# One core, retention feeding a hypermixer: another order of loads, steps, engines and banks, pair 4 loaded in 256-byte rows, and the last half pair projected in two column halves

## The chip, the core and the metric

The kernel runs on one core of one Trainium2 chip. The core has five engines that run side by side, each with a queue of its own: TensorE (PE, with its weight loads shown apart as PEld), VectorE (DVE), ScalarE (ACT), GpSimd (POOL) and SyncE (SP, which here only issues transfers). The metric is the time of one execution on the device, in microseconds. The kernel before took 95.64 us, the median of three runs (94.63 to 96.15).

## The reference

Two parts follow each other. With B = 4 batches, H = 8 heads, S = 768 steps and D = 64, the first is a linear attention with a decaying state, the second a token mixer on its result, which has 512 columns (8 heads of 64):

```python
gamma = 1.0 - 2.0 ** (-5.0 - np.arange(H))
for t in range(S):
    state = gamma * state + einsum('bhd,bhe->bhde', k[:, :, t], v[:, :, t])
    y[:, :, t] = scale * einsum('bhd,bhde->bhe', q[:, :, t], state)
x = y.transpose(0, 2, 1, 3).reshape(B, S, H * D)
wq, wk = x @ w_q, x @ w_k                       # 512 -> 64
W_tok = scale * einsum('bsd,btd->bst', wq, wk)
mixed = einsum('bst,btd->bsd', W_tok, x)
out = np.maximum(mixed, 0.0) @ w_out            # 512 x 512
```

Inputs and output are float32; the engines compute in bfloat16 with float32 sums.

## The kernel before, in words

The 4 x 768 tokens are cut into 12 **pairs** of two chunks of 128 tokens, three pairs to a batch. Each pair goes through the same steps, and every step is a small function (L450 to L981) named by two or three letters:

- **Loads** (`load`, L157): q, k and v of a pair, 512 KB each, into a pool of 16 staging buffers. A pair of type "1" has k and v loaded by one transfer each, two tokens in a row of 512 bytes; a pair of type "n" by two transfers each, one for each chunk, a token of a head in a row of 256 bytes. q comes in rows of 2 KB. `TYPES` (L63) gives each pair's type. SP issues the loads in the order of `LOADS` (L58); a load waits until the cast that reads its buffer's last content, 16 loads back, is done (`more_loads`, L227). `w` holds w_q and w_k, `o0` and `o1` the halves of w_out. `s3` stores pair 3's output, `s9/1` chunk 1 of pair 9; the stores all stand behind the loads.
- **Casts to bfloat16**: `ck`, `cv` (with the decay factors), `cq`. For type "1" each half of a chunk is an instruction on 64 partitions, two for a chunk; for type "n" one instruction on 128. [...]
- **Transposes** on PE, `trk`, `trq`, `xt`, and their evictions `ek`, `eq`, `exT`. Where `HALVED` (L64) has a 1, a transpose is made as two halves of 64 rows into two banks of PSUM in place of one.
- **Attention**: `sc` (q times k, two halves of the heads), `eat` (evict under the causal mask, on DVE), `ia` (masked scores times v), `in` (q times the state of before), `st` and `es` (state update and its eviction), `ex` (evict x).
- **Mixer**: `wk`, `wq`, `ew` (x times w_k and w_q, evicted), `zm`, `ez` (sum of wk times x over a batch, evicted: so the rest of a batch waits for its last pair), `mx`, `r` (wq times that sum, and the relu), `pj`, `eo` (times w_out, evicted to the output buffer). The last pair, 11, is in `SPLIT`: most of its steps run for each chunk apart.

`ORDER` (L16) writes the whole program out by hand: 430 tokens such as `sc.3.1@5` (pair 3, half 1, into bank 5 of the 8 PSUM banks) or `ek.5:V` (on DVE; A is ACT, P is POOL). Each engine runs its own tokens in that order; between engines only data and buffers make one wait. `fill.8@6` are 8 matmuls of 512 columns on zeros, which keep PE busy where it would wait. `W` and `WO.0`, `WO.1` cast the weights; `pj` needs both `WO`.

The diff touches the tables at the top, `pj` (L963), `eo` (L975), `stored` (L985) and the first loads (L220).

Of the kernel before, what the change touches and what calls it, by code (L numbers as in the profile page):

```python
# [64 lines left out]
TWO_WQ = "0000"  # L65
DECAYED_Q = "000000111001"
# [993 lines left out]
```

## Time and profile before

| | us |
|---|---|
| median of three runs | 95.64 |
| profiled execution, its own time | 95.0 |
| its span in the profile | 93.3 |
| PE busy | 85.2 |
| DVE busy | 72.7 |
| ACT busy | 67.4 |
| POOL busy | 65.1 |

A profile's line "L966 PE MATMUL banks<-wout_sb,relu" is a group: line 966 of the kernel, on PE, reading tiles wout_sb and relu and writing PSUM (the tile `banks`). A row of a timeline has the start, the duration, the engine, the line, the operation, and in brackets how long the engine sat idle ahead of it and for what. "SPq" is SP's queue: the issue of a transfer, waits of the queue included. Releasers are inferred, and a wait for several things is put down to the one that came last. A matmul's end is modelled, so the time between the starts of two groups on PE says more than a group's own duration; the chain of work (start, duration, engine, line, number of matmuls) cuts PE's time up without overlap.

### The profile page before, as it was taken

What the parts mean: (1) busy time and instruction counts of PE and PEld (TensorE: products, weight loads), DVE (VectorE), ACT (ScalarE), POOL (GpSimd) and SP (SyncE); (2) the same over time, 40 slices, a digit from 0 to 9 for tenths busy, and PEclk for the clock granted to TensorE, in tenths of its full rate; (3) what the DMA queues carried; (4) which work ended last, traced back from release to release, by engine and by line L of the source; (5) the groups of instructions that cost most, each with busy time, mean ns of one, the idle gap of its engine ahead of it and who ended that gap; (6) DMA issues with size and microseconds to landing.
All of it is one profiled execution on the core that took longest, in us unless ns stands there. A gap on an engine that the chain in (4) does not pass through costs nothing.

```text
span 93.3 us, 3399 instructions
## 1 busy us (share of the span) xinstructions
PE 85.2 (91%) x1406; PEld 55.4 (59%) x1420; DVE 72.7 (78%) x116; ACT 67.4 (72%) x107; POOL 65.1 (70%) x84
## 2 busy tenths in 40 slices
PE   4997999898999999999999999999999999999940
PEld 1353566656887764578777557768774586744410
DVE  4869679979899999798798978988898894433730
ACT  4284479995969989877949889888678598367220
POOL 7879699999999999999998699978559500000000
PEclk9999999999999999999999999999999999999999
DMA  1999999999999999897998996998999999935683
GB/s 22 264 376 379 358 369 332 274 311 359 370 372 348 339 262 314 228 258 176 303 207 241 359 291 134 317 241 234 274 209 296 403 404 400 399 120 202 263 313 122
DMA packets 43567, 26.69 MB, mean 286 GB/s; under 512 B 22560, under 2 KB 36896, under 8 KB 43552
## 3 DMA queue, kind: packets, MB, share of 16 engines
q1 hardware_dynamic: 43024, 26.22, 92.8%
q10 hardware_dynamic: 528, 0.26, 0.9%
q8 instruction: 11, 0.18, 0.7%
q14 instruction: 4, 0.03, 0.1%
HBM read 20.19 MB, written 6.29 MB: 284 GB/s over the span
## 4 chain that ended last, share of the span: by engine, by line
PE 66%; SPq 15%; DMA 7%; DVE 4%; issue 2%; ACT 2%; DVEq 0%
PE banks L966 23%; DMA q_st<-in_q_dram 7%; SPq L186 6%; PE banks L594 6%; PE banks L826 5%; SPq L164 5%; PE banks L697 5%; PE banks L665 4%; PE banks L802 4%; SPq L202 4%; PE banks L878 3%; PE banks L514 3%; PE banks L651 3%; DVE x_nat L740 3%; PE banks L770 2%; PE banks L569 2%
## 5 line engine op out<-in xcount | busy, mean ns | idle before, releaser
L467 POOL TENSOR_TENSOR vs<-v_st,fv 64x512 bf16<-64x512 f32 x26 | 28.1, 1082 | 2.5 <-DMA v_st<-in_v_dram 1.0
L966 PE MATMUL banks<-wout_sb,relu 128*128 128x512 bf16 x85 | 22.5, 380 | 0.8 <-issue 0.3
L608 DVE TENSOR_TENSOR at_sb<-banks,cmask 128x1024 bf16<-128x1024 f32 x14 | 16.6, 1220 | 1.5 <-PE banks L594 0.9
L148 ACT COPY o_st<-banks 128x512 f32<-128x512 f32 x21 | 12.3, 589 | 7.3 <-PE banks L966 7.1
L608 DVE TENSOR_TENSOR at_sb<-banks,cmask_n 128x1024 bf16<-128x1024 f32 x10 | 12.0, 1221 | 1.9 <-PE banks L594 1.1
L149 POOL CAST ks<-k_st 64x512 bf16<-64x512 f32 (+1 forms) x20 | 12.1, 609 | 1.6 <-DMA k_st<-in_k_dram 1.0
L966 PEld LDWEIGHTS <-relu 128*128 128x128 bf16 x96 | 8.1, 98 | 8.5 <-DVE relu L961 0.5
L148 ACT CAST s_sb<-banks 128x512 bf16<-128x512 f32 x17 | 10.0, 586 | 3.2 <-PE banks L665 3.0
L444 PE MATMUL banks<-warm 128*128 128x512 bf16 x33 | 10.6, 453 | 1.6 <-DVE warm L253 1.3
L148 ACT CAST ks<-k_st 64x512 bf16<-64x512 f32 (+1 forms) x16 | 9.9, 620 | 2.4 <-DMA k_st<-in_k_dram 2.3
L740 DVE TENSOR_TENSOR x_nat<-banks,fy 128x1024 bf16<-128x1024 f32 x8 | 9.8, 1222 | 2.1 <-PE banks L697 1.2
L959 ACT ACTIVATE relu<-banks 128x1024 bf16<-128x1024 f32 (+1 forms) x11 | 10.2, 946 | 0.9 <-PE banks L938 0.9
L488 POOL TENSOR_TENSOR vs<-v_st,fn_n 128x512 bf16<-128x512 f32 x8 | 8.2, 1042 | 1.9 <-DMA v_st<-in_v_dram 1.9
L594 PE MATMUL banks<-qT,kT 64*128 64x128 bf16 x192 | 9.2, 218 | 0.2 <-DVE x_nat L740 0.2
L534 POOL TENSOR_TENSOR qs<-q_st,fq 128x1024 bf16<-128x1024 f32 x4 | 7.6, 1911 | 1.0 <-DMA q_st<-in_q_dram 1.0
L149 DVE COPY kT<-banks 128x1024 bf16<-128x1024 bf16 x11 | 7.6, 688 | 0.9 <-PE banks L514 0.7
L594 PEld LDWEIGHTS <-kT 64*128 64x128 bf16 x192 | 5.6, 94 | 4.3 <-issue 2.2
L697 PE MATMUL banks<-vs,at_sb 128*128 128x64 bf16 x176 | 7.8, 194 | 0.1
L665 PE MATMUL banks<-vs,ks 128*128 128x128 bf16 x80 | 7.8, 220 | 0.0
L149 DVE COPY xT<-banks 128x1024 bf16<-128x1024 bf16 (+1 forms) x10 | 6.3, 634 | 1.8 <-PE banks L768 1.3
L697 PEld LDWEIGHTS <-at_sb 128*128 128x128 bf16 x176 | 6.3, 98 | 2.1 <-issue 0.6
L148 ACT CAST wqk_n<-banks 128x384 bf16<-128x384 f32 (+1 forms) x12 | 5.5, 470 | 2.3 <-PE banks L826 2.0
(88 smaller groups left out, 140.9 us busy)
## 6 DMA issues: line engine op xcount, KB each, us to landing
q_st<-in_q_dram SPq DMA_DIRECT2D x12, 512.0 KB, 6.8
out_dram<-o_st SPq DMA_DIRECT2D x9, 512.0 KB, 5.2
v_st<-in_v_dram SPq DMA_DIRECT2D x7, 512.0 KB, 6.7
k_st<-in_k_dram SPq DMA_DIRECT2D x6, 512.0 KB, 6.1
k_st<-in_k_dram SPq DMA_DIRECT2D x11, 256.0 KB, 5.1
v_st<-in_v_dram SPq DMA_DIRECT2D x10, 256.0 KB, 5.4
out_dram<-o_st SPq DMA_DIRECT2D x6, 256.0 KB, 2.0
o_st<-in_moe_w_out_dram SPq DMA_DIRECT2D x2, 512.0 KB, 9.4
```

Of the source, the lines that this page charges most:

```text
L148: return nc.scalar.copy(out=out, in_=in_)
L149: return ENGINES[e].tensor_copy(out=out, in_=in_)
L444: nc.tensor.matmul(out=bank32(b), lhsT=warm[:, 0:128], rhs=warm, start=True, stop=True)
L467: ENGINES[e].tensor_tensor(out=st["vs"][rows(j), c].rearrange("p hp x d -> p (hp x) d"), in0=st["v_st"][rows(c), :, :, j].rearrange("p hp ...
L488: ENGINES[e].tensor_tensor(out=st["vs"][:, c].rearrange("p hp x d -> p (hp x) d"), in0=st["v_st"][:, c].rearrange("p hp x d -> p (hp x) d" ...
L594: nc.tensor.matmul(out=ps[:, x, hi, c, :], lhsT=st["kT"][rows(x), hp, c, :], rhs=qT(p, x, hp, c), start=(hi == 0 and c == 0), stop=(hi == ...
L608: ENGINES[e].tensor_tensor(out=st["at", half].rearrange("p x hi i t -> p (x hi i t)").rearrange("p (m n) -> p m n", n=n), in0=st["at_ps", ...
L665: nc.tensor.matmul(out=state_ps(p)[:, hp].rearrange("p x d -> p (x d)"), lhsT=st["ks"][:, c, hp].rearrange("p x d -> p (x d)"), rhs=st["vs ...
L697: nc.tensor.matmul(out=y_of(p, b, c)[:, x, hp, :], lhsT=st["at", half][:, x, hi, c, :], rhs=st["vs"][:, c, hp, x, :], start=first(p, x), s ...
L740: nc.vector.tensor_tensor(out=st["x"].rearrange("p c hp x d -> p x (c hp) d"), in0=st["y_ps", 0].rearrange("p x c hp d -> p x (c hp) d"), ...
L959: nc.scalar.activation(out=dst, in_=src, func=ACT.Relu)
L966: nc.tensor.matmul(out=bank32(b), lhsT=st["relu"][:, c, a, :], rhs=wout_sb[:, a, :], start=(a == 0), stop=(a == NDM - 1),)
```

## The change

It keeps every function's arithmetic. These things differ:

- **ORDER** is another one, of 436 tokens. All steps of before are in it, in other places, many with another bank or engine. `fill` has 34 matmuls for 36. `cq.2`, `cq.7` and `cq.8` are split in halves, and of the two halves of pairs 4 and 8 one runs on DVE. `WO.1` moves from POOL to ACT.
- **LOADS** is another order: k1 ahead of v1, q3 and k3 ahead of w, k5 ahead of q4 and k4, o1 next behind k4; q5 and v4 behind o1.
- **TYPES**: pair 4 is "n" now, so its k and v come in 256-byte rows by four transfers, and its casts are one instruction for each chunk.
- **HALVED**: k for pairs 0, 8, 9, 10, 11 (before 5, 10); q for 0, 5, 8, 10, 11 (before 0, 5, 7 to 11); x for 4, 5, 7 to 10 (before 4, 6, 7, 9 to 11).
- **DECAYED_Q**: pairs 4, 5, 8, 10, 11 (before 6, 7, 8, 11).
- **The last half pair**: `pj.11.0`, `eo.11.0` and the store of pair 11's first chunk are cut into two halves of 256 columns and come last; the second half's store is issued from ACT's queue.
- `FIRST` is a new switch for the first loads, and it is empty, so the first loads stay.

```diff
-mask.0:P mask.2:P fill.13@6 cv.0.1:V ck.0.1:P ck.0.0:A fx:A trk.0@0 ek.0:V cq.0:A fill.8@6 trq.0@1
-eq.0:V fill.4@6 sc.0.1@0 cq.1.0:A cv.0.0:P st.0.0 es.0.0:A sc.0.0@2 fill.2@6 st.0.1 eat.0.1:V
-in.0.1@0 ia.0.1@0 eat.0.0:V cq.1.1:P fill.2@6 ia.0.0@0 ex.0:V trq.1@2 cv.1.1:P ck.1.0:A ck.1.1:P
-trk.1@3 ek.1:V cq.2:A trq.2@6 eq.2:V eq.1:A fill.2@5 sc.1.0@2 eat.1.0:V xt.0@0 sc.1.1@5 es.0.1:A
-cv.1.0:P st.1.0 ck.2.1:A eat.1.1:V ck.2.0:P fill.1@4 trk.2@1 es.1.0:A st.1.1 in.1.0@2 ia.1.0@2
-ek.2:V cv.2.0:P ia.1.1@2 W:A in.1.1@2 es.1.1:A ck.3.0:A ex.1:V sc.2.1@4 eat.2.1:V fill.3@6 sc.2.0@1
-eat.2.0:V cv.2.1:P xt.1@3 ck.3.1:P cq.3:A fill.1@6 st.2.0 es.2.0:A ia.2.1@4 exT.0:A trq.3@6 in.2.1@4
...
-ez.0.0:V mx.0@2 r.0:A mx.2@4 r.2:A ck.4.0:P trq.4@6 ex.3:V xt.3@0 WO.0:P eq.4:V trq.5@1 cv.4.1:P
-exT.3:V eq.5:A trk.4@6 ek.4:V wk.3@0 st.3.1 es.3.1:V mx.1@3 r.1:A sc.4.0@5 eat.4.0:V sc.4.1@1 wq.3
-ew.3:A WO.1:P pj.2.1@3 pj.1.1@0 ck.5.0:A eo.2.1:A eo.1.1:A pj.0.1@6 cv.4.0:P st.4.0 es.4.0:A
...
-pj.10.0@0 mx.10.1@3 r.10.1:V mx.11.1@1 r.11.1:V eo.10.0:A pj.9.0@6 eo.9.0:A pj.10.1@3 eo.10.1:V
-pj.11.1@6 pj.9.1@1 eo.9.1:A eo.11.1:V
+mask.0:P mask.2:P fill.13@6 cv.0.0:V ck.0.0:A ck.0.1:P fx:A trk.0@0 ek.0:V cq.0:A fill.8@6 trq.0@2
+cq.1.1:A cv.0.1:P fill.1@6 st.0.0 es.0.0:A eq.0:V fill.1@6 sc.0.0@1 eat.0.0:V sc.0.1@3 in.0.1@5
+eat.0.1:V cq.1.0:P st.0.1 trq.1@0 ia.0.0@5 ck.1.1:A ck.1.0:P trk.1@1 ek.1:V fill.1@2 ia.0.1@5 ex.0:V
+eq.1:A fill.1@4 sc.1.1@0 eat.1.1:V fill.4@4 xt.0@6 sc.1.0@4 eat.1.0:V cv.1.1:P es.0.1:A ck.2.1:A
+ck.2.0:A trk.2@3 ek.2:V cv.1.0:P cq.2.1:P st.1.0 cq.2.0:A trq.2@0 eq.2:V cv.2.0:P ia.1.0@4 es.1.0:A
+exT.0:A ia.1.1@4 st.1.1 es.1.1:A in.1.1@4 in.1.0@4 fill.1@3 sc.2.0@0 sc.2.1@2 ex.1:V fill.2@6 xt.1@4
+cq.3:A cv.2.1:P fill.2@6 st.2.0 trq.3@5 ck.3.1:A es.2.0:A eat.2.1:V ia.2.1@2 W:A in.2.1@2 in.2.0@2
...
+st.3.0 es.3.0:A zm.2@2 zm.1@2 ez.0.0:A eat.3.1:V cq.4.0:V ia.3.0@3 in.3.1@3 mx.2@1 r.2:A ia.3.1@3
+st.3.1 WO.1:A mx.1@5 ex.3:V r.1:A cq.4.1:P trq.4@0 eq.4:V WO.0:P ck.4.0:P ck.4.1:P trk.4@1 ek.4:V
+xt.3@3 pj.2.1@4 eo.2.1:A exT.3:V sc.4.0@0 ck.5.1:P es.3.1:V mx.0@5 r.0:A eat.4.0:V pj.1.1@2 eo.1.1:A
...
+r.9.1:V pj.9.1@6 eo.9.1:V mx.11.0@1 r.11.0:V mx.11.1@3 pj.10.1@0 eo.10.1:V r.11.1:A pj.11.1@6
+pj.11.0.0@5 eo.11.1:V eo.11.0.0:A pj.11.0.1@1 eo.11.0.1:A
...
-v0 q0 q1 v1 k1 q2 k2 v2 w k3 q3 v3 q4 q5 k4 o0 v4 o1 k5 v5 q6 k6 q7 v6 k7 k8 v7 q8 v8 q9 k9 q11 k11
-v9 q10 k10 v10 v11a v11b s0 s2 s1 s4 s3 s5 s6 s8 s7 s11/0 s10/0 s9/0 s10/1 s11/1 s9/1
+v0 q0 q1 k1 v1 k2 q2 v2 q3 k3 w v3 k5 q4 o0 k4 o1 q5 v4 q6 v5 k6 k8 v6 q7 q8 k7 v7 v8 k9 q9 v9 q10
+k10 q11 k11 v10 v11a v11b s1 s2 s0 s3 s4 s5 s8 s7 s6 s10/0 s9/0 s9/1 s10/1 s11/1 s11/0/0 s11/0/1
...
-TYPES = "111111nn1nnn"
-HALVED = dict(k="000001000010", q="100001011111", x="000010110111")
+TYPES = "1111n1nn1nnn"
+HALVED = dict(k="100000001111", q="100001001011", x="000011011110")
...
-DECAYED_Q = "000000111001"
+DECAYED_Q = "000011001011"
...
-    def pj(e, b, p, c):
+    def columns(half):
+        return slice(0, DM) if half is None else slice(half * DM // 2, (half + 1) * DM // 2)
+
+    def pj(e, b, p, c, half=None):
         st = pairs[p]
+        cols = columns(half)
+        ps = bank32(b)[:, 0 : cols.stop - cols.start]
         for a in range(NDM):
             nc.tensor.matmul(
-                out=bank32(b),
+                out=ps,
                 lhsT=st["relu"][:, c, a, :],
-                rhs=wout_sb[:, a, :],
+                rhs=wout_sb[:, a, cols],
...
-        copy(e, st["o"][:, c], st["o_ps", c])
-        evicted.add((p, c))
+        copy(e, st["o"][:, c, columns(half)], st["o_ps", c, half])
+        evicted.add((p, c, half))
...
-            nc.sync.dma_start(out=out[b, t0 : t0 + C, :], in_=pairs[p]["o"][:, cs[0]])
+            (nc.scalar if half else nc.sync).dma_start(
+                out=out[b, t0 : t0 + C, columns(half)],
+                in_=pairs[p]["o"][:, c, columns(half)],
+            )
```

More of the change, by code (lines that the diff above doesn't have):

```diff
@@ L218, in load_token, with load_chunk @@
             load(token[0], int(token[1:]))
-    load("k", 0, 0, nc.scalar)
-    load("k", 0, 1, nc.sync)
-    queue = list(LOADS)
-    staged = ["k0"]
+    def load_chunk(name, c, eng):
+        st = pairs[0]
+        if name + "_st" not in st:
+            st[name + "_st"] = stage_pool.tile([128, HP, 2, 2, D], FP32, name=name + "_st", tag="st")
+        eng.dma_start(
+            out=st[name + "_st"][rows(c)].rearrange("g hp x j d -> g (hp x) (j d)"),
+            in_={"k": k, "v": v}[name][0, :, c * C : (c + 1) * C, :].rearrange(
+                "h (g j) d -> g h (j d)", j=2
+            ),
+        )
+    if FIRST:
+        for i, piece in enumerate(FIRST.split()):
+            load_chunk(piece[0], int(piece[1]), nc.sync if i else nc.scalar)
+        staged = ["k0", "v0"]
+    else:
+        load("k", 0, 0, nc.scalar)
+        load("k", 0, 1, nc.sync)
+        staged = ["k0"]
+    queue = list(LOADS)[len(staged) - 1 :]
     cast = set()
@@ L972, in pj, with eo @@
             )
-        st["o_ps", c] = bank32(b)
-    def eo(e, b, p, c):
+        st["o_ps", c, half] = ps
+    def eo(e, b, p, c, half=None):
         st = pairs[p]
@@ L985, in stored @@
     def stored(name):
[L986 to L988 removed]
+        p, c, half = ([int(i) for i in name.split("/")] + [None, None])[:3]
+        if not all((p, i, half) in evicted for i in ([0, 1] if c is None else [c])):
             return False
         b, cp = divmod(p, NP)
[L991 to L993 removed]
+        if c is not None:
+            t0 = (2 * cp + c) * C
+            (nc.scalar if half else nc.sync).dma_start(
+                out=out[b, t0 : t0 + C, columns(half)],
+                in_=pairs[p]["o"][:, c, columns(half)],
+            )
         else:
```

58 lines of the change are left out of this document (27 added, 31 removed).

## The prediction

> **What bounds the kernel now.** I read the page first: the span, the busy shares, the slices.
>
> ```profile
> span 93.3 us, 3399 instructions
> PE 85.2 (91%) x1406; PEld 55.4 (59%) x1420; DVE 72.7 (78%) x116; ACT 67.4 (72%) x107; POOL 65.1 (70%) x84
> PE   4997999898999999999999999999999999999940
> DMA  1999999999999999897998996998999999935683
> ```
>
> PE and the DMA queues look full together, DVE comes next. Second, the table of stretches (us, then busy time and count of PE, PEld, DVE, ACT, POOL, clock, DMA share, GB/s), to see how much PE idles once the first loads are in.
>
> ```profile
> 20.00:30.00 10.00, 9.34 (x175) 7.29 (x176) 9.14 (x10) 8.09 (x14) 9.37 (x12) 1.00 1.07 360
> 30.00:40.00 10.00, 9.70 (x154) 6.00 (x154) 9.01 (x11) 9.07 (x14) 9.45 (x10) 1.00 1.01 291
> 40.00:50.00 10.00, 9.86 (x193) 7.46 (x195) 8.81 (x9) 7.39 (x13) 9.74 (x11) 1.00 0.94 218
> 50.00:60.00 10.00, 9.84 (x180) 6.39 (x181) 8.99 (x11) 8.88 (x14) 8.72 (x10) 1.00 1.01 286
> 60.00:70.00 10.00, 9.88 (x233) 7.48 (x231) 8.43 (x10) 7.99 (x14) 7.10 (x8) 1.00 1.02 243
> 70.00:80.00 10.00, 9.74 (x209) 6.68 (x209) 8.01 (x11) 7.41 (x13) 3.63 (x4) 1.00 1.07 377
> ```
>
> From 30 to 80 us PE idles 0.30 + 0.14 + 0.16 + 0.12 + 0.26 = 1.0 us of 50, at full granted clock. So no order can win more than about 1 us there, and any new wait is paid in full. What is left to win is ahead of 22 us, where PE runs filler matmuls, and behind the last matmul.
>
> Third, the loads: SP's queue, the transfer rates in two stretches of one microsecond (10 to 11, rows of 512 bytes; 59 to 60, rows of 256 bytes), and the last load's reader.
>
> ```profile
> DMA packets 681, 0.35 MB, mean 347 GB/s; under 512 B 4, under 2 KB 681, under 8 KB 681
> DMA packets 1095, 0.29 MB, mean 290 GB/s; under 512 B 1087, under 2 KB 1087, under 8 KB 1095
> 23.76 3.90 SPq L206 DMA_DIRECT2D o_st<-in_moe_w_out_dram  x1
> o_st<-in_moe_w_out_dram SPq DMA_DIRECT2D x1, 512.0 KB, 8.9
> 30.41 2.29 SPq L164 DMA_DIRECT2D q_st<-in_q_dram  x1
> 63.58 5.83 SPq L176 DMA_DIRECT2D v_st<-in_v_dram  x4
> 73.30 1.04 POOL L488 TENSOR_TENSOR vs<-v_st,fn_n 128x512 bf16<-128x512 f32 x1 [0.71 <-DMA v_st<-in_v_dram]
> ```
>
> A tensor of one pair (0.524 MB) takes 0.524/0.347 = 1.51 us in rows of 512 bytes and 0.524/0.290 = 1.81 us in rows of 256. From 30.41 to 69.41 SP issues 28 load transfers, one per 1.39 us, whether of 256 or 512 KB. The last one is used as it lands (0.71 us idle ahead of it): the loads are a second bound with almost no slack.
>
> **The change, part by part.** Nearly every step of the order is the same step in another place. I take the places that move the end.
>
> *The front.* DVE leads here; the first four rows are its own, the others PE's.
>
> ```profile
> 10.94 2.36 DVE L608 TENSOR_TENSOR at_sb<-banks,cmask 128x1024 bf16<-128x1024 f32 x2 [0.68 <-PE banks L594]
> 13.87 1.23 DVE L740 TENSOR_TENSOR x_nat<-banks,fy 128x1024 bf16<-128x1024 f32 x1 [0.57 <-PE banks L697]
> 18.61 0.69 DVE L149 COPY kT<-banks 128x1024 bf16<-128x1024 bf16 x1
> 19.86 1.23 DVE L740 TENSOR_TENSOR x_nat<-banks,fy 128x1024 bf16<-128x1024 f32 x1 [0.56 <-PE banks L651]
> 21.13 0.38 PE L594 MATMUL banks<-qT,kT 64*128 64x128 bf16 x7 [0.18 <-DVE x_nat L740]
> 21.45 0.62 PE L770 MATMUL banks<-identity,x_nat 128*128 128x128 bf16 x8
> 21.90 0.38 PE L444 MATMUL banks<-warm 128*128 128x512 bf16 x1
> 22.12 0.39 PE L665 MATMUL banks<-vs,ks 128*128 128x128 bf16 x4
> ```
>
> DVE twice waits for PE, 0.57 and 0.56 us, because PE came late to ia and in behind fills. In the new order k1 is loaded ahead of v1, trq.1 and trk.1 follow sc.0.1 at once, and ek.1 stands ahead of ex.0 on DVE, so it fills the first wait; ek.2 and eq.2 stand together ahead of ex.1 and fill the second. From the end of pair 0's masks (10.94 + 2.36 = 13.30) the new DVE chain is ek.1 0.69, ex.0 1.23, two masks 2.36, ek.2 and eq.2 1.38, ex.1 1.23: 6.89, so ex.1 ends at 20.2. Now it ends at 19.86 + 1.23 = 21.1. Both orders then run xt.1, fills and st.2.0, which is PE's row at 22.12. Now sc.2.0 also waits for ex.1 (0.18 idle, then 0.32 until 21.45); in the new order it has other banks and runs earlier. New: 20.2, xt.1 0.45 (21.45 to 21.90), two fills of 0.22 (21.90 to 22.12): st.2.0 at 21.1, 1.0 us earlier. I take -0.85, leaving 0.15 for handovers. Ends: -1.13 (both waits gone) and -0.44 (only the two fills gone by which the whole order is shorter, 34 for 36).
>
> *Pair 4 and the output weights.* Pair 4's k and v now come as four transfers of 256 KB in 256-byte rows in place of two of 512 KB; o1, the second half of w_out, is asked for after k4. WO.1, its cast, goes from POOL to ACT and stands ahead of r.1 there; trk.4, xt.3 and pj.2.1 stand earlier on PE. Rows of now: the cast, the first projection, an ACT cast of that size, and the steps that pj.2.1 is moved past, from the chain of work.
>
> ```profile
> 33.82 1.04 POOL L149 CAST wout_sb<-o_st 128x1024 bf16<-128x1024 f32 x1
> 34.77 2.76 PE L966 MATMUL banks<-wout_sb,relu 128*128 128x512 bf16 x11
> L148 ACT CAST qs<-q_st 128x1024 bf16<-128x1024 f32 x3 | 3.1, 1046 | 2.1 <-DMA q_st<-in_q_dram 2.0
> 31.91 0.34 PE banks L569 x16
> 32.25 0.55 PE banks L514 x8
> 32.80 0.30 PE banks L802 x8
> 33.32 0.33 PE banks L938 x4
> 33.65 0.56 PE banks L594 x16
> 34.21 0.54 PE banks L826 x4
> ```
>
> pj.2.1 now starts as WO.1 ends, with no wait. The new order takes from ahead of it trq.5 (0.34), wk.3 (0.30), wq.3 (0.54), both sc.4 (0.56) and one mx (4 + 4 matmuls, about 0.45): 2.2 us. PE would be there at 34.77 - 0.85 - 2.2 = 31.7. o1 lands now at 23.76 + 8.9 = 32.66. In the new list q5 and v4 no longer stand ahead of it and k5 does: one tensor less (-1.51), k4 in smaller rows (+0.30), so 31.45; ACT's cast takes 1.05, so wout is there at 32.5. PE waits 0.8 us. Behind WO.1 on ACT stand r.1 and with it mx.0's bank and pj.1.1; sc.4.0 and mx.0 cover r.1's microsecond. I take +0.8; ends 0 (o1 0.8 earlier) and +2.0 (o1 no earlier than now, since it is the 21st transfer in both lists). Of v4: 0.30 more, its reader is later, nothing. The rest of pair 4 saves POOL and ACT instructions, with PE as cover: nothing.
>
> What 256-byte rows cost is 290 against 347 GB/s in the rows above, a sixth. [...]
>
> *PE's own work.* k is transposed in halves for five pairs in place of two, q for five in place of seven, x for six in both. Full and halved k are above and below here (0.55; 0.34), full and halved q likewise (0.62; 0.34).
>
> ```profile
> 23.06 0.62 PE banks L571 x8
> 37.76 0.34 PE banks L510 x16
> ```
>
> 2 x 0.28 - 3 x 0.21 = -0.07: nothing. A halved transpose fills two banks; where the other is still being read it waits, which is in the open term below.
>
> *Engines changed elsewhere.* ACT, POOL and DVE steps are traded (three eq more and two ek fewer on DVE, decayed q halves there, ez all on ACT). Summed by their rows DVE loses about 0.4 us, ACT 1, POOL 2.5. None sets the end as long as PE is fed: nothing, with PE's 1.0 us of idle (30 to 80 us) as the most that could be won, and the loss open.
>
> *The last half pair.* Rows of now: eviction, store, and an ACT eviction of 256 columns.
>
> ```profile
> 89.68 0.59 ACT o_st L148
> 90.30 0.33 SPq L993 DMA_DIRECT2D out_dram<-o_st  x1
> out_dram<-o_st SPq DMA_DIRECT2D x1, 256.0 KB, 2.0
> L148 ACT CAST z_sb<-banks 128x256 bf16<-128x256 f32 x2 | 0.7, 372 | 1.3 <-PE banks L878 1.3
> ```
>
> The two half projections stream the same columns through PE: nothing. The last eviction shrinks from 0.59 to 0.37 (-0.22). The last store has 128 KB for 256; I take 0.13 off its 2.0 us (ends 0 and 0.45), since most of that is not bytes. It is issued from ACT, behind nothing. Chunk 11.1 is evicted on DVE while PE runs the two halves, so its store is not the last. Sum -0.35, ends -0.67 and 0.
>
> **Sum**: -0.85 + 0.8 + 0 - 0.35 = -0.4 us. The profiled execution took 95.0 us (1.7 beyond its span), so 94.6; the median of the runs is 95.64, 1% above that.
>
> **Rivals.**
>
> *B, the loads set the pace (slower).* If a transfer costs its turn of 1.39 us and not its bytes, o1, 21st in both lists, still lands at 32.66, WO.1 ends at 33.7, and PE waits 2.0 us ahead of pj.2.1: 95.0 - 0.85 + 2.0 - 0.35 = 95.8, and later loads come 2 x 1.39 = 2.8 us later, v6 being wanted earlier than now; 1 us lost there gives 96.8. For it: the 1.39 us over 28 transfers, the DMA share near 1. Against: rows of 512 bytes fill the queue at 347 GB/s in the front, where bytes count. It decides from a wait of 1.2 us on there; below that the change is not slower.
>
> *C, the front's gain stays (faster).* o1 lands by 30.7, there is no new wait, and the middle gives back 0.4 of its 1.0 us: 95.0 - 0.85 - 0.35 - 0.4 = 93.4. For it: DVE and POOL have less to do. Against: the loads have no slack, as the 0.71 us at 73.30 shows.
>
> *D, nothing happens.* PE's work is the same within 0.1 us, and gains and waits cancel: 95.0 to 95.6. It lies inside my range and is not told apart from the forecast.
>
> **How the numbers follow.** Forecast with D 0.45, B 0.30, C 0.25. The forecast is 94.6, its own range 93.8 to 95.6. About 2% is what a measurement of this kernel can tell: below 93.7 and above 97.6. Of C four fifths and a little of the forecast are faster: 0.23. Of B about two fifths, and some other lost wait, are slower: 0.15. The rest, 0.62, is the same. The range to hold 8 in 10 goes from C (93.4, with the tail's far end 93.0) to B with a second wait, 96.8.
>
> **What would show it.** DVE's ex.1 (L740) should end near 20.2 and st.2.0 (L665) start near 21.3. A wait of near 0.8 us ahead of the first L966 group, behind ACT's cast of wout_sb, which waits for the DMA of o_st, shows the second step; none there speaks for C, 2 us for B. The last ACT o_st should take 0.37 us with some 3.3 us from PE's end to the span's. PE idle of over 2 us between 35 and 80 us in the table of stretches, or POOL waiting for v_st ahead of pair 6, would make the prediction wrong towards slow.

## The result and the profile after

The changed kernel is slower: 97.12 us median of 20 runs against 95.65 us of 20 runs of the kernel before, a ratio of 1.0127 with the 95% interval 1.0091 to 1.0163. The medians are over all executions, while the ratios, here and below, leave out those that ran slow, so the two need not agree. The difference is under the 2% that the prediction took as what a measurement of this kernel can tell, but its interval lies clear of 1. The forecast was 0.4 us less (94.6 us against the profiled 95.0); 1.0127 x 95.0 = 96.2 us is what came, 1.2 us more. The profiled execution of the changed kernel took 96.14 us with a span of 94.4 us (before: 95.0 and 93.3).

In the line numbers of the changed kernel, the matmuls of `pj` are L990, those of `st` L684, of `sc` L613, of `trk` L533 (L529 in halves); POOL's casts of v are L486 (type "1") and L507 (type "n"); copies are L149 on ACT and L150 on DVE and POOL; `ex` is L759.

First the page of the changed kernel: the span, the busy sums, and from the 40 slices PE, the granted clock and the DMA queues.

```profile
span 94.4 us, 3420 instructions
PE 84.5 (90%) x1415; PEld 56.8 (60%) x1430; DVE 71.8 (76%) x116; ACT 67.2 (71%) x107; POOL 63.4 (67%) x84
PE   4999978999957999999999999999979999999940
PEclk9999999999999589999999999999999999999999
DMA  0999999999998999999999989999989999965863
```

PE's work is the same (84.5 for 85.2 us), the DMA queues are as full as before, and there are two new things in the middle: a 5 and a 7 in PE's slices behind 26 us, and a stretch of lower granted clock behind it. The table of stretches (us, then busy time and count of PE, PEld, DVE, ACT, POOL, clock, DMA share, GB/s), with its sum from 10 to 80 us, shows the size:

```profile
20.00:30.00 10.00, 7.87 (x145) 6.33 (x145) 8.94 (x10) 7.26 (x14) 8.08 (x9) 1.00 0.97 283
30.00:40.00 10.00, 9.89 (x123) 6.40 (x122) 6.92 (x9) 7.09 (x11) 8.68 (x11) 0.83 1.09 297
40.00:50.00 10.00, 9.95 (x229) 7.82 (x230) 9.12 (x12) 8.00 (x14) 8.08 (x10) 1.00 1.06 281
...
60.00:70.00 10.00, 9.31 (x220) 6.92 (x221) 8.40 (x10) 8.40 (x14) 7.13 (x8) 1.00 1.06 259
...
sum 70.00, PE 65.54 PEld 47.53 DVE 58.86 ACT 56.06 POOL 55.20; mean PE 9.36 PEld 6.79 DVE 8.41 ACT 8.01 POOL 7.89
```

The same sum for the kernel before:

```profile
sum 70.00, PE 67.59 PEld 47.58 DVE 60.59 ACT 56.83 POOL 56.74; mean PE 9.66 PEld 6.80 DVE 8.66 ACT 8.12 POOL 8.11
```

PE idles 70 - 65.54 = 4.46 us between 10 and 80 us, where it idled 2.41. (Three of the profiles below that differ little from this order, and that kept the full clock, have 4.2 to 4.7.) The front itself did what was forecast; these are DVE's `ex.1` and PE's `st.2.0`, the rows to hold against 19.86 and 22.12 of before:

```profile
18.85 1.22 DVE L759 TENSOR_TENSOR x_nat<-banks,fy 128x1024 bf16<-128x1024 f32 x1 [0.34 <-PE banks L670]
...
21.02 0.39 PE L684 MATMUL banks<-vs,ks 128*128 128x128 bf16 x4
```

`ex.1` ends at 20.07 and `st.2.0` starts 1.10 us earlier. The gain lasts until 27 us. Rows of SP's queue, POOL and PE in the changed kernel show where it ends:

```profile
16.31 0.67 SPq L203 DMA_DIRECT2D w_st<-in_moe_w_k_dram  x1
17.02 1.55 SPq L187 DMA_DIRECT2D v_st<-in_v_dram  x1
...
24.55 4.35 POOL L486 TENSOR_TENSOR vs<-v_st,fv 64x512 bf16<-64x512 f32 x4 [1.50 <-DMA v_st<-in_v_dram]
...
28.95 0.38 PE L684 MATMUL banks<-vs,ks 128*128 128x128 bf16 x4 [1.77 <-POOL vs L486]
```

And the rows of the kernel before for the same load, casts and `st.3.0`:

```profile
17.28 0.60 SPq L186 DMA_DIRECT2D v_st<-in_v_dram  x1
...
23.74 4.37 POOL L467 TENSOR_TENSOR vs<-v_st,fv 64x512 bf16<-64x512 f32 x4
...
27.90 0.39 PE L665 MATMUL banks<-vs,ks 128*128 128x128 bf16 x4
```

v3 is asked for at the same moment in both (17.02 and 17.28), since the same transfers stand ahead of it. In the kernel before, POOL takes it at 23.74 without a wait. In the changed one POOL is ready at 23.04 and sits 1.50 us until 24.55, and PE waits 1.77 us for POOL. PE ran ahead by 1.1 us; the load did not. Of POOL's 1.50 us, though, only 0.6 are POOL's being ready earlier (23.04 for 23.66). The rest is this load: it landed 7.5 us behind its issue, in the kernel before 6.2. In five other profiles below with the same loads ahead of v3 it landed after 5.5 to 6.7 us, and PE waited 0.35 to 1.04 us at `st.3.0`, so the 1.77 us of this one execution are more than the usual price. The rest of the way the changed kernel shows the same pattern in smaller pieces, at the casts of v6, v9 and q11, and on PE behind q11's:

```profile
44.33 2.04 POOL L507 TENSOR_TENSOR vs<-v_st,fn_n 128x512 bf16<-128x512 f32 x2 [1.10 <-DMA v_st<-in_v_dram]
...
61.43 2.04 POOL L507 TENSOR_TENSOR vs<-v_st,fn_n 128x512 bf16<-128x512 f32 x2 [1.23 <-DMA v_st<-in_v_dram]
...
68.13 1.90 POOL L553 TENSOR_TENSOR qs<-q_st,fq 128x1024 bf16<-128x1024 f32 x1 [1.35 <-DMA q_st<-in_q_dram]
...
70.08 0.41 PE L588 MATMUL banks<-identity_q,qs 64*128 64x64 bf16 x16 [0.51 <-POOL qs L553]
...
66.23 4.99 SPq L177 DMA_DIRECT2D v_st<-in_v_dram  x4
```

The last row is SP's queue: the last loads are issued by 71.22 us, 1.8 us later than before.

### The profile page after: what moved, and what is told of

Same layout as the page of the kernel before. It is cut to its first block, busy times and chain, and to the rows that moved or that the text cites. A ratio compares the mean times of both kernels' runs of the same rounds, so it can differ in the third digit from the quotient of the medians.

```text
span 94.4 us, 3420 instructions
## 1 busy us (share of the span) xinstructions
PE 84.5 (90%) x1415; PEld 56.8 (60%) x1430; DVE 71.8 (76%) x116; ACT 67.2 (71%) x107; POOL 63.4 (67%) x84
## 4 chain that ended last, share of the span: by engine, by line
PE 55%; DMA 16%; POOL 16%; issue 5%; SPq 3%; ACT 0%; POOLq 0%
PE banks L990 21%; POOL vs L486 12%; DMA v_st<-in_v_dram 9%; DMA q_st<-in_q_dram 8%; PE banks L613 4%; PE banks L684 4%; PE banks L716 4%; PE banks L845 3%; PE banks L957 3%; PE banks L897 2%; PE banks L533 2%; PE banks L590 2%; POOL qs L553 2%; PE banks L670 2%; PE banks L821 2%
## 5 line engine op out<-in xcount | busy, mean ns | idle before, releaser
L486 POOL TENSOR_TENSOR vs<-v_st,fv 64x512 bf16<-64x512 f32 x22 | 23.8, 1083 | 3.3 <-DMA v_st<-in_v_dram 2.2
L990 PE MATMUL banks<-wout_sb,relu 128*128 128x512 bf16 (+1 forms) x88 | 22.5, 371 | 0.8 <-issue 0.3
L149 ACT COPY o_st<-banks 128x512 f32<-128x512 f32 (+1 forms) x20 | 11.3, 565 | 6.5 <-PE banks L990 6.2
L627 DVE TENSOR_TENSOR at_sb<-banks,cmask_n 128x1024 bf16<-128x1024 f32 x12 | 14.3, 1214 | 0.8 <-PE banks L613 0.8
L627 DVE TENSOR_TENSOR at_sb<-banks,cmask 128x1024 bf16<-128x1024 f32 x12 | 14.1, 1217 | 1.0 <-PE banks L613 0.6
L150 POOL CAST ks<-k_st 64x512 bf16<-64x512 f32 (+1 forms) x21 | 13.0, 629 | 1.7 <-DMA k_st<-in_k_dram 1.1
L990 PEld LDWEIGHTS <-relu 128*128 128x128 bf16 x100 | 8.5, 98 | 8.3 <-issue 0.6
L507 POOL TENSOR_TENSOR vs<-v_st,fn_n 128x512 bf16<-128x512 f32 x11 | 11.3, 1042 | 2.7 <-DMA v_st<-in_v_dram 2.7
L149 ACT CAST s_sb<-banks 128x512 bf16<-128x512 f32 x17 | 10.0, 587 | 3.7 <-PE banks L684 3.6
L149 ACT CAST ks<-k_st 64x512 bf16<-64x512 f32 (+1 forms) x15 | 9.3, 618 | 3.2 <-DMA k_st<-in_k_dram 3.0
L759 DVE TENSOR_TENSOR x_nat<-banks,fy 128x1024 bf16<-128x1024 f32 x7 | 8.5, 1221 | 2.8 <-PE banks L716 2.2
L684 PE MATMUL banks<-vs,ks 128*128 128x128 bf16 x80 | 8.0, 224 | 1.9 <-POOL vs L486 1.8
L553 POOL TENSOR_TENSOR qs<-q_st,fq 128x1024 bf16<-128x1024 f32 (+1 forms) x5 | 8.1, 1624 | 1.8 <-DMA q_st<-in_q_dram 1.6
L150 DVE COPY xT<-banks 128x1024 bf16<-128x1024 bf16 (+1 forms) x11 | 7.0, 640 | 2.8 <-PE banks L787 1.5
L150 DVE COPY qT<-banks 128x1024 bf16<-128x1024 bf16 x10 | 6.9, 688 | 2.3 <-PE banks L588 1.0
L613 PE MATMUL banks<-qT,kT 64*128 64x128 bf16 x192 | 8.5, 217 | 0.0
L684 PEld LDWEIGHTS <-ks 128*128 128x128 bf16 x80 | 5.4, 100 | 3.4 <-issue 2.1
L613 PEld LDWEIGHTS <-kT 64*128 64x128 bf16 x192 | 5.8, 94 | 2.6 <-issue 1.5
```

The costliest lines, as they stand in the source:

```text
L149: return nc.scalar.copy(out=out, in_=in_)
L150: return ENGINES[e].tensor_copy(out=out, in_=in_)
L486: ENGINES[e].tensor_tensor(out=st["vs"][rows(j), c].rearrange("p hp x d -> p (hp x) d"), in0=st["v_st"][rows(c), :, :, j].rearrange("p hp ...
L507: ENGINES[e].tensor_tensor(out=st["vs"][:, c].rearrange("p hp x d -> p (hp x) d"), in0=st["v_st"][:, c].rearrange("p hp x d -> p (hp x) d" ...
L553: ENGINES[e].tensor_tensor(out=st["qs"][:, js].rearrange("p j x d -> p x j d"), in0=st["q_st"][:, :, js], in1=fq[:, :, p % NP, js].to_broa ...
L613: nc.tensor.matmul(out=ps[:, x, hi, c, :], lhsT=st["kT"][rows(x), hp, c, :], rhs=qT(p, x, hp, c), start=(hi == 0 and c == 0), stop=(hi == ...
```

## The experiments

The ratios are to the kernel before, run beside it on the same chip. "Late loads" below is the theory that the changed order wants its loads earlier than they come, and that pair 4's small rows make that worse.

### v3 ahead of the w transfers; the wait filled

The nearest reading was that the one wait at `st.3.0`, or the lower clock behind it, is the whole loss. Two kernels take these away, one each, from the changed kernel:

```diff
-... k2 q2 v2 q3 k3 w v3 k5 ...
+... k2 q2 v2 q3 k3 v3 w k5 ...
```

> The changed kernel with v3 loaded ahead of w, nothing else. Theory V (v3 comes about 1 us late behind the two transfers of w, POOL waits for it, PE waits 1.8 us at st.3.0 and its clock then halves): POOL's 1.5 us wait for v_st near 24.5 us falls under 0.4, PE's wait ahead of st.3.0 under 0.5, the clock stays at 1.0 from 20 to 40 us, and the time falls by 1.0 to 2.0 us, to a ratio of 0.99 to 1.002 to the kernel before. Theory S (pair 4's 256-byte rows, two transfers more, starve every later load): the wait at st.3.0 goes, but the time falls by at most 0.4 us, ratio 1.008 to 1.014, since PE waits later instead.

Measured: 97.16 us, ratio 1.0149 (1.0092 to 1.0206). The wait at `st.3.0` shrank to 0.34 us, and nothing was won: the table of stretches has PE at 9.41 from 20 to 30 us and at 8.32 from 40 to 50.

```profile
40.00:50.00 10.00, 8.32 (x206) 6.76 (x200) 7.82 (x10) 7.05 (x12) 7.96 (x9) 1.00 1.02 274
...
42.26 0.62 ACT L149 CAST ks<-k_st 128x512 bf16<-128x512 f32 x1 [0.76 <-DMA k_st<-in_k_dram]
...
42.93 0.56 PE L533 MATMUL banks<-identity,ks 128*128 128x128 bf16 x7 [1.23 <-ACT ks L149]
```

`trk.6` now waits 1.23 us for ACT's cast of k6, and ACT for the load, 0.76 us at the second half (1.29 at the first). The place of v3 is not the cause; removing one wait moves it to the next load.

```diff
-... ew.2:A zm.0@2 cv.3.0:P st.3.0 ...
+... ew.2:A zm.0@2 cv.3.0:P fill.8@1 st.3.0 ...
```

> The changed kernel with 8 filler matmuls (about 1.7 us) in the place where PE waits ahead of st.3.0. Theory G (the halved clock behind the idle stretch is what costs): the clock stays at 1.0 from 30 to 34 us, and the time falls by 0.7 to 1.2 us in spite of the wait. The rival, that the wait itself is the whole loss and PE catches up behind the slow stretch: no change, within 0.4 us.

Measured: 97.14 us, ratio 1.0119 (1.0045 to 1.0192), granted clock 1.00 from 0 to 80 us in its profile. The fills alone prove little, since in that profile POOL waited only 0.28 us for v3. The executions of the changed kernel say more: the profiled one has a mean granted clock of 0.982, the 19 others have 0.992 or more, and it is the second fastest of the 20. The lower clock is not what makes the changed kernel slow.

### Pair 4 in full rows; the tail whole

```diff
-TYPES = "1111n1nn1nnn"
+TYPES = "111111nn1nnn"
```

> The changed kernel with pair 4 in 512-byte rows again (type 1), all orders kept. Theory S: later loads come up to 2.8 us earlier, the 0.5 us wait ahead of trq.11 goes, and the time falls by 1 us or more, ratio under 1.003. Theory V: v3 stands ahead of pair 4 in the list, so the 1.8 us wait at st.3.0 and the halved clock stay; POOL pays 1.2 us more for casts; ratio 1.008 to 1.018.

Measured: 96.5 us, ratio 1.0043 (0.9969 to 1.0118): the first part of the change whose undoing seems to help, but the interval still reaches the changed kernel's. The loads move clearly: the last ones are issued by 68.64 us, 2.6 us earlier than in the changed kernel.

```diff
-... pj.11.1@6 pj.11.0.0@5 eo.11.1:V eo.11.0.0:A pj.11.0.1@1 eo.11.0.1:A
+... pj.11.1@6 pj.11.0@5 eo.11.1:V eo.11.0:A
-... s11/1 s11/0/0 s11/0/1
+... s11/1 s11/0
```

> The changed kernel with the last half pair in one piece again (pj.11.0, eo.11.0 and its store whole, still last, store from SP). My prediction counted 0.35 us for the halves: the time would rise by that, and the time from the last matmul to the end from 3.6 to 4.0 us. The rival, that the smaller last transfer from ACT's queue takes as long as a whole one from SP's, expects 0.0 to 0.2 us.

Measured: 97.1 us, ratio 1.0056 (0.9971 to 1.0141), which can't tell. Its trace shows more, the last rows of PE and ACT:

```profile
88.51 2.76 PE L990 MATMUL banks<-wout_sb,relu 128*128 128x512 bf16 x12
...
91.31 0.59 ACT L149 COPY o_st<-banks 128x512 f32<-128x512 f32 x1 [2.03 <-PE banks L990]
```

PE ends at 91.27 and the span at 95.0, 3.73 us later; in halves, by the rows shown in the section on why the prediction was wrong, it was 94.4 - 90.75 = 3.65. The halves are worth less than 0.1 us.

### One part alone, in the order before

```diff
-TYPES = "111111nn1nnn"
+TYPES = "1111n1nn1nnn"
```

> The kernel before with one part of the change alone: pair 4 of type n, 256-byte rows in four transfers; all orders as before. Theory S (the loads are the bound, and pair 4's four transfers delay all loads behind them): SP issues the last load 1.5 to 3 us later than 69.4 us, the last cast on POOL starts 1 to 3 us later than 73.3, and the time rises by 0.8 to 2 us, ratio 1.008 to 1.02. Its rival, that the new orders are the loss: no change, 0.997 to 1.004, POOL being 1.2 us freer.

Measured: 95.66 us, ratio 0.9972 (0.9921 to 1.0022). In the old order the small rows of pair 4 cost nothing.

```diff
+        elif token in ("k4", "v4"):
+            for half in range(2):
+                load(token[0], 4, half)
```

> The kernel before with pair 4's k and v still in 512-byte rows, but each in two transfers of 256 KB (four heads each). It tells apart two forms of theory S. If a transfer costs its turn in SP's queue (1.39 us whatever its size): as much later as with the 256-byte rows, the last load issued 1.5 to 3 us later, ratio 1.008 to 1.02. If rows and bytes cost: nothing, ratio 0.996 to 1.004.

Measured: 95.92 us, ratio 1.001 (0.9968 to 1.0051). Two more transfers of 256 KB with the same bytes in 512-byte rows cost nothing either: that a transfer costs its turn, whatever its size, is not so where 256 KB are concerned. The last load is issued by 69.84 us, 0.4 us later than in the kernel before, where two turns of 1.39 us would have made it 2.8.

```diff
-pj.11.1@6 pj.9.1@1 eo.9.1:A eo.11.1:V
+pj.11.1@6 pj.9.1.0@1 eo.11.1:V eo.9.1.0:A pj.9.1.1@3 eo.9.1.1:A
-... s11/1 s9/1
+... s11/1 s9/1/0 s9/1/1
```

> The kernel before with its own last projection, pj.9.1, in two column halves, the second stored from ACT's queue; all else as before. My prediction's term: 0.35 us less. What the two traces of the changed kernel say (91.31 to 95.0 whole, 90.79 to 94.4 in halves): 0.1 us less, not to be told from none, ratio 0.995 to 1.003.

(The kernel also has the changed kernel's lines for `pj`, `eo` and the stores, which make the halves possible.)

Measured: 95.44 us, ratio 0.9946 (0.9905 to 0.9986). The old order with its last half pair in two column halves is faster by about 0.5%. Its trace doesn't show where. PE's last row:

```profile
86.94 3.64 PE L990 MATMUL banks<-wout_sb,relu 128*128 128x512 bf16 x19
```

From PE's last matmul (90.58) to the span's end (94.2) it is 3.6 us, as in the kernel before (93.3 - 89.65 = 3.65). This stays open.

### v3 early and pair 4 in full rows, then k4's cast

```diff
-... k2 q2 v2 q3 k3 w v3 k5 ...
+... k2 q2 v2 q3 k3 v3 w k5 ...
-TYPES = "1111n1nn1nnn"
+TYPES = "111111nn1nnn"
```

> The changed kernel with pair 4 in 512-byte rows and v3 ahead of w. If theory S is the whole of it: as with the rows alone, ratio 1.000 to 1.008. If the wait at st.3.0 costs something once the loads are no longer late: 0.5 to 1.5 us better than with the rows alone, ratio 0.988 to 0.998.

Measured: 95.84 us, ratio 1.002 (0.9979 to 1.0061). Against the kernel with v3 early alone (1.0149, 1.0092 to 1.0206) the only edit is pair 4's row size, and the intervals don't meet: in the new order the small rows cost 1.3%, with some 0.7% of noise either way (the two kernels were measured on different chips, each beside the kernel before). The same edit without v3's move, from 1.0127 to 1.0043, points the same way. What PE waited for in this kernel is one cast of twice as many instructions:

```profile
31.33 0.23 PE L533 MATMUL banks<-identity,ks 128*128 128x128 bf16 x1 [0.59 <-POOL ks L150]
32.66 0.56 PE L533 MATMUL banks<-identity,ks 128*128 128x128 bf16 x7 [1.10 <-POOL ks L150]
```

So half of that cast went to ACT, which idled there:

```diff
-... st.3.1 WO.1:A mx.1@5 ...
+... st.3.1 ck.4.0:A WO.1:A mx.1@5 ...
-... WO.0:P ck.4.0:P ck.4.1:P trk.4@1 ...
+... WO.0:P ck.4.1:P trk.4@1 ...
```

> The changed order with v3 ahead of the w transfers and pair 4 in 512-byte rows (95.84 us, ratio 1.002 in the run before), and now the first half of k4's cast on ACT ahead of WO.1 instead of on POOL behind WO.0. Theory K (with full rows only POOL's casts of k4 still cost: PE waited 0.59 and 1.10 us for them at trk.4): trk.4 comes about 1.3 us earlier and PE has no wait of that size until 69, so the time is about 94.5 us, ratio 0.985 to 0.99 to the kernel before. Theory R (the new order as such loses time, whatever single wait is taken out, because the next engine is as late): a wait of the same size comes up at pj.2.1 or behind, and the time stays at 95.6 to 96.0, ratio 1.00.

Measured: 95.11 us, ratio 0.9945 (0.991 to 0.9979), faster than both kernels. The gain over the kernel it comes from is 0.75%, some 0.7 us, about half of what was expected. Some of it goes with the clock: of the ten executions from which that kernel's ratio comes, three have a mean granted clock of 0.979 to 0.982 and took 96.30 to 96.52 us, the seven others have 0.992 or more and took 95.27 to 95.86; with the cast on ACT all twelve have 0.995 or more. In the trace `trk.4` still waits 0.81 us, now for ACT, and `pj.2.1` 0.39 us for WO.1, whose load is late:

```profile
31.67 0.62 PE L533 MATMUL banks<-identity,ks 128*128 128x128 bf16 x8 [0.81 <-ACT ks L149]
...
33.56 0.59 PE L990 MATMUL banks<-wout_sb,relu 128*128 128x512 bf16 x2 [0.39 <-ACT wout_sb L149]
```

### Another pair in full rows

```diff
-TYPES = "1111n1nn1nnn"
+TYPES = "1111n11n1nnn"
```

> The changed kernel with pair 6 in 512-byte rows instead of 256-byte rows; pair 4 keeps the small rows, so that there are as many small-row pairs as in the kernel before. Theory S (the slower loads of one more small-row pair reach every later cast): the last load is issued at about 69.5 to 70 us instead of 71.2, POOL's waits for v7, q11 shrink, and the time falls by 0.5 to 1 us to about 96.2, ratio about 1.005. Rival P (it is pair 4 alone, by its place behind the front, that costs): the time stays within 0.3 us of the changed kernel's 97.1, ratio 1.013.

(What the expectation calls v7's wait is v9's in the order.)

Measured: 97.26 us, ratio 1.0135 (1.0084 to 1.0186). Late loads in their simple form (count the small-row pairs) fail here. The last load is issued by 68.09 us, 3.1 us earlier than in the changed kernel, and nothing is won:

```profile
61.59 6.50 SPq L177 DMA_DIRECT2D v_st<-in_v_dram  x4
...
44.02 4.37 POOL L486 TENSOR_TENSOR vs<-v_st,fv 64x512 bf16<-64x512 f32 x4 [1.28 <-DMA v_st<-in_v_dram]
...
43.10 0.56 PE L533 MATMUL banks<-identity,ks 128*128 128x128 bf16 x7 [0.95 <-ACT ks L149]
...
51.47 0.20 PE L529 MATMUL banks<-identity,ks 64*128 64x64 bf16 x1 [0.46 <-POOL ks L150]
52.14 0.37 PE L529 MATMUL banks<-identity,ks 64*128 64x64 bf16 x13 [0.47 <-POOL ks L150]
```

Full rows make the casts of a pair longer: v6 on POOL takes 4.37 us in four instructions for 2.04 in two, and PE waits for POOL and ACT where it gained at the loads. v6 itself is still waited for, 1.28 us. A pair's type trades cast time against load time, and which one counts depends on the place.

The same edit in the faster kernel, the one with k4's cast on ACT:

```diff
-TYPES = "111111nn1nnn"
+TYPES = "1111111n1nnn"
```

> The kernel of the k4 cast on ACT, with pair 6 in 512-byte rows too (four small-row pairs instead of five). Theory S, if the loads are still what the later casts wait for: another 0.3 to 0.6 us less than that kernel, about 94.1. If the loads no longer limit there once pair 4 has full rows: within 0.2 us of that kernel, or later by what POOL's longer casts of pair 6 cost (four of 1.09 us in place of two of 1.02 us for v6).

Measured: 95.89 us, ratio 1.004 (1.0002 to 1.0077), 1% slower than with pair 6 in small rows: the same trade, lost again.

### One load less, in three orders

The most direct test takes 512 KB out of the queue and moves nothing else by hand. It leaves out the load of o1, and `WO.1` casts o0's buffer a second time:

```diff
-... k4 o1 q5 v4 ...
+... k4 q5 v4 ...
+        if token == "o0":
+            wstages["o1"] = st
```

> The changed kernel without the load of o1, the second half of the output weights (512 KB): WO.1 casts the buffer of o0 instead, so the second half of the output projection uses the wrong rows; everything else is unchanged, pair 4 keeps its small rows. Theory S: all loads behind o1 come 1.2 to 1.6 us earlier, the waits for DMA behind 40 us go, and the time falls by about 1 us to 96.0, ratio about 1.003. Theory R (engines and steps of the new order cost the time, the loads do not): the time stays at 97 us, ratio 1.01 to 1.016.

Measured: 95.21 us, ratio 0.9869 (0.983 to 0.9909). By the ratios the changed order falls by 2.6%, some 2.5 us, more than twice what was expected, and ends clearly below the kernel before (the executions behind the ratio average 94.4 us, the kernel before 95.6).

The same lines in the kernel before:

```diff
-... o0 v4 o1 k5 ...
+... o0 v4 k5 ...
+        if token == "o0":
+            wstages["o1"] = st
```

> The kernel before without the load of o1 (WO.1 casts the buffer of o0, so the second half of the output projection uses the wrong rows). Theory S (the changed order wants its loads earlier than they can come, the order before does not): the time stays within 0.5 us of the kernel before, ratio 0.995 to 1.0, against 2.5 us in the changed order. Rival C (the loads are a common limit of both orders, and the loss has another cause): it falls by 1.5 us or more, ratio 0.985 or less.

Measured: 95.68 us, ratio 1.003 (0.9994 to 1.0067). The old order gains nothing from the same edit. The two sums of the stretches from 10 to 80 us, the changed order's first, and the last loads of SP's queue in the same order:

```profile
sum 70.00, PE 67.90 PEld 48.59 DVE 60.46 ACT 57.12 POOL 55.37; mean PE 9.70 PEld 6.94 DVE 8.64 ACT 8.16 POOL 7.91
64.27 4.80 SPq L177 DMA_DIRECT2D v_st<-in_v_dram  x4
```

```profile
sum 70.00, PE 68.01 PEld 47.05 DVE 61.84 ACT 56.75 POOL 57.52; mean PE 9.72 PEld 6.72 DVE 8.83 ACT 8.11 POOL 8.22
59.47 5.94 SPq L176 DMA_DIRECT2D v_st<-in_v_dram  x4
```

In the changed order PE's idle time falls from 4.46 to 2.10 us, in the old one from 2.41 to 1.99, although there the loads are done at 65.41 in place of 69.41 us. The loads limit the new order and not the old one, and that is enough to account for the loss. Two other readings of this test do not fit. Leaving out o1 also frees `WO.1` from a wait, but PE did not wait for `WO.1` in the changed kernel, and the old order has the same relief and no gain. It also lets each later load have its staging buffer one cast sooner, but v7, which takes v3's buffer, is issued at 45.28 us in the changed kernel, 16 us after v3's cast (24.55 + 4.35 = 28.90).

And in the kernel with k4's cast on ACT:

```diff
-... k4 o1 q5 v4 ...
+... k4 q5 v4 ...
+        if token == "o0":
+            wstages["o1"] = st
```

> The kernel with v3 early, pair 4 in full rows and half of k4's cast on ACT, without the load of o1 (the same rows wrong). Theory S: with full rows the loads are no longer what the casts wait for, except WO.1's own 0.84 us and POOL's 1.06 us for q5: 94.3 to 94.8 us, ratio 0.987 to 0.992. Rival C: it falls by the same 2.5 us as in the changed kernel, to 92.6, ratio 0.97.

Measured: 94.37 us, ratio 0.9893 (0.9842 to 0.9943), 0.5% below the kernel with o1, and the intervals overlap. With pair 4 in full rows little of the time hangs on that load.

### What is left of the k4 fix

```diff
-... k2 q2 v2 q3 k3 v3 w k5 ...
+... k2 q2 v2 q3 k3 w v3 k5 ...
```

> The changed kernel with pair 4 in full rows and half of k4's cast on ACT, v3 left behind the w transfers. If v3's place matters by the waits that the traces show at st.3.0 (1.77 us in the changed kernel's profile, 0.35 to 0.89 in five others of the same order, 0.34 with v3 early): 0.3 to 0.6 us slower than with v3 early, 95.4 to 95.7, ratio 0.998 to 1.001. If it does not matter: 95.1, ratio 0.9945.

Measured: 95.28 us, ratio 0.997 (0.9925 to 1.0015). v3's place is worth at most a few tenths; the two kernels' intervals overlap. The wait at `st.3.0` in this profile is 1.04 us, with v3 early 0.34:

```profile
28.30 0.38 PE L684 MATMUL banks<-vs,ks 128*128 128x128 bf16 x4 [1.04 <-POOL vs L486]
```

```diff
-... mx.2@1 r.2:A ia.3.1@3 st.3.1 ck.4.0:A WO.1:A ... WO.0:P ck.4.1:P trk.4@1 ... xt.3@3 pj.2.1@4 ... sc.4.0@0 ...
+... mx.2@1 ck.4.0:A r.2:A ia.3.1@3 st.3.1 WO.1:A ... ck.4.1:P WO.0:P trk.4@1 ... xt.3@3 sc.4.0@0 ... pj.2.1@4 ...
```

> The kernel with v3 early, pair 4 in full rows and half of k4's cast on ACT, with both halves of k4's cast one place earlier on their engines (ahead of r.2 on ACT, ahead of WO.0 on POOL) and pair 4's first scores ahead of pj.2.1 on PE. Theory K (what is left at trk.4, 0.81 us, is a wait for the place of the cast): trk.4 starts about 0.8 us earlier, pj.2.1's wait for WO.1 is covered by the scores, and the time falls by 0.5 to 0.8 us to about 94.5, ratio 0.987. Theory R: r.2, WO.0 or the loads behind them are as late as the casts were, and the time stays at 95.1, ratio 0.9945.

Measured: 95.54 us, ratio 0.9958 (0.9918 to 0.9998), no better than without the edit. `trk.4` starts at 31.86 for 31.67:

```profile
31.86 0.61 PE L533 MATMUL banks<-identity,ks 128*128 128x128 bf16 x8 [1.19 <-ACT relu L978]
```

It writes bank 1, which `mx.2@1` filled and `r.2` has to read first, and `r.2` now stands behind the cast. The edit exchanged the wait for the cast for one for the bank.

## Why the prediction was wrong

**The front (-0.85): right.** `ex.1` was put at 20.2 and came at 20.07; `st.2.0` was put 1.0 us earlier and came 1.10 earlier.

**Pair 4 and the output weights (+0.8): the wait came, but not there, and it was only one of several.** WO.1's cast and the first projection in the changed kernel:

```profile
32.34 1.05 ACT L149 CAST wout_sb<-o_st 128x1024 bf16<-128x1024 f32 x1 [0.31 <-DMA o_st<-in_moe_w_out_dram]
...
34.60 0.81 PE L990 MATMUL banks<-wout_sb,relu 128*128 128x512 bf16 x3
```

o1 was put at 31.45 and landed at 32.34, near its old 32.66, 0.9 us late. The projection did not wait for it, since PE had lost 1.77 us at `st.3.0` before and more in the slow stretch behind it. Nor did it in the kernels with v3 early, the tail whole or pair 6 in full rows, where PE lost 0.3 to 0.9 us at `st.3.0` and 0.3 at `trk.4`. The working looked for the wait at the one place where the order of loads had been changed by hand, and asked nowhere whether loads that keep their place, like v3, come as early as a PE that has gained 1.1 us wants them.

**"Of v4: nothing" and "the rest of pair 4: nothing", with 0.30 us as the price of a tensor in small rows: the step that failed.** PE was named as the cover. The prediction's own reading was that the loads are a second bound with almost no slack; with that, what k4 and v4 take longer is not hidden but goes on to every later load. The price itself was too small. It came from a rate of 290 GB/s in one microsecond (59 to 60), and among the microseconds of the kernel before with over 95% small packets none is faster. Over four microseconds of small rows (66 to 70) and four of larger ones (24 to 28) the same profile has:

```profile
DMA packets 3605, 0.92 MB, mean 231 GB/s; under 512 B 3604, under 2 KB 3604, under 8 KB 3604
...
DMA packets 1787, 1.45 MB, mean 364 GB/s; under 512 B 46, under 2 KB 1434, under 8 KB 1785
```

That is 0.524/0.231 = 2.27 us for a tensor against 1.44, an estimate of 0.8 us more for each. The prediction's count of 28 transfers says still more. They carry 8 tensors in larger rows and 10 in small ones: 8 x 1.51 + 10 x 1.81 = 30.2 us by its prices, and they took 39.0, as if a small tensor took 1.2 us more, not 0.30 (an estimate that takes the queue as never standing still). With 1.2 us for k4 the same working has o1 at 32.35; it landed at 32.34 here, and at 31.5 to 32.1 in the kernels with v3 early, the tail whole or pair 6 in full rows. The runs agree. The last loads are issued by 71.22 us in the changed kernel and by 68.64 with pair 4 in full rows, 2.6 us apart where 2 x 0.30 had been counted. In the four profiles of the changed order with pair 4 in small rows and all else loaded they are issued by 71.2 to 72.5, in four of the five with pair 4 in full rows and pair 6 in small ones by 68.6 to 69.3 (the fifth has 71.2). The small rows cost 1.3% of the time where the kernels differ in nothing else (v3 early, with and without them), and nothing in the old order. In the new one each load is wanted earlier, so the same lateness is a wait there.

**Engines elsewhere ("nothing, the loss open"): the rule beside it held, the size was missed.** No order could win more than the 1.0 us of idle, and any new wait is paid. It was: PE's idle time between 10 and 80 us grew by 2.05 us. Of the two signs that were named for "wrong towards slow", POOL waiting for v_st ahead of pair 6 is there (1.10 us at 44.33); PE's idle time between 35 and 80 us is not, at 1.2 us for the 2 that were named, since most of the loss in this execution came before 35 us.

**PE's own work (0): right**, 84.5 us busy for 85.2.

**The last half pair (-0.35): half of the working held.** The changed kernel's last rows of PE, ACT and ACT's queue, and the landing times of the stores:

```profile
87.98 2.77 PE L990 MATMUL banks<-wout_sb,relu 128*128 128x512 bf16 x15
...
90.35 0.81 ACT L149 COPY o_st<-banks 128x256 f32<-128x256 f32 x2 [1.61 <-PE banks L990]
91.19 0.36 ACTq L1016 DMA_DIRECT2D out_dram<-o_st  x1
...
out_dram<-o_st SPq DMA_DIRECT2D x5, 256.0 KB, 2.0
...
out_dram<-o_st SPq DMA_DIRECT2D x1, 128.0 KB, 1.9
out_dram<-o_st ACTq DMA_DIRECT2D x1, 128.0 KB, 2.1
```

PE's last row in the kernel before:

```profile
86.02 3.63 PE L966 MATMUL banks<-wout_sb,relu 128*128 128x512 bf16 x15
```

The last eviction ends 91.16 - 90.75 = 0.41 us behind PE, before 90.27 - 89.65 = 0.62: the -0.22 is there. The store did not get shorter with its bytes: from its issue to the span's end it took 94.4 - 91.19 = 3.2 us, before 93.3 - 90.30 = 3.0. The sum is nothing, the near end of the range given.

**The rivals.** B named the mechanism, loads that set the pace, and its time, 95.8 to 96.8, holds the 96.2 that came. Its 2.8 us by which later loads come later is near the 2.6 above. Its form was off: it put the price on the count of transfers, and two more transfers of the same bytes cost nothing. The 2.0 us of wait ahead of pj.2.1 in its sum are not there either, so that its time fits is in part luck. By the prediction's sign, no wait there spoke for C, the rival that was furthest off. B got 0.30 where the forecast got 0.45, because the forecast weighed the loads' lack of slack against C only, and not against itself.

## What to carry to other kernels

When a change makes one engine run ahead, write down for every load behind that place when it is asked for and when its first reader will now be ready: an edit that leaves a load where it was still makes it late. If loads and the busiest engine are full together, a gain on the one is only real as far as the other has slack, and leaving one transfer out, in both orders, tells in one measurement each which of them limits. The choice of row size is a trade of load time against cast time, and is to be made anew for each place in the order, with a rate taken over several microseconds and not from one: here it cost 1.3% at pair 4, and undoing it at pair 6 gained nothing.

## What the hardware showed

- **The granted clock.** In the profiled execution of the changed kernel the clock was at half for 3.4 us behind the idle stretch at `st.3.0` (from 30.35 to 33.77, as the mean clocks of 0.85 from 30.0 to 30.5 us and 0.73 from 33.5 to 34.0 give it), after PE had idled 1.77 us at a stretch. Most of that stretch:

```profile
30.50:33.50 3.00, 3.00 (x31) 2.00 (x28) 1.25 (x2) 2.18 (x3) 2.89 (x5) 0.50 1.07 324
```

The kernel with v3 early and pair 4 in full rows, whose waits of 0.59 and 1.10 us with one matmul between are shown above, has it too, a little behind them, and again for 3.4 us (from 33.50 to 36.92, worked out the same way from the clocks of 0.75, 0.50, 0.50 and 0.54 in these rows):

```profile
33.00:34.00 1.00, 0.78 (x13) 0.72 (x12) 0.67 (x2) 0.25 (x1) 0.89 (x2) 0.75 1.08 383
34.00:35.00 1.00, 1.00 (x3) 0.22 (x2) 1.00 (x3) 0.00 (x0) 0.98 (x1) 0.50 1.07 351
35.00:36.00 1.00, 1.00 (x13) 0.56 (x12) 0.23 (x2) 0.56 (x1) 1.00 (x2) 0.50 1.14 319
36.00:37.00 1.00, 1.00 (x6) 0.28 (x3) 1.00 (x1) 0.62 (x2) 0.93 (x2) 0.54 0.78 194
```

But the changed kernel with pair 4 in full rows has nearly the same waits in its profile (0.55 and 1.10 us with one matmul between) and kept the full clock there (a mean of 1.000). So the length of the idle time alone does not decide it, and what does stays open. The kernel with the wait of 1.04 us at `st.3.0` kept the full clock in its profile too (1.000), and so did the one with fills in the wait (1.000), which was no faster.

- **Small stores.** 128 KB from ACT's queue took 2.1 us to land, 128 KB from SP's 1.9 and 256 KB from SP's 2.0. In these rows halving the bytes changes nothing that shows: the 0.13 us that the prediction took off for them is not there.

- **Rows of 256 bytes.** The two single microseconds of the kernel before gave a ratio of the rates, rows of 256 bytes to rows of 512, of 290/347 = 0.84. The four microseconds each that are shown above gave 231/364 = 0.63.
